# Batch 0 of an attention and mixer kernel: first loads split by token range and head, scores of four heads at a time

## The chip, the cores and the metric

The kernel runs on one core of a Trainium2 chip. The metric is the device time of one execution in microseconds. Engines are named as in the profile: PE does matmuls (PEld is its weight load), DVE works on vectors, ACT on activations, POOL and SP here issue DMAs.

## What is computed

```python
# q, k, v: (8 batches, 8 heads, 576 tokens, 64), f32
scores = scale * np.matmul(q, k.transpose(0, 1, 3, 2))
mask = block_i >= block_j                 # blocks of 64 tokens
attn = softmax(np.where(mask, scores, -1e9))
x = np.matmul(attn, v)                    # then (batch, token, 512)
h = np.maximum(x.T @ w_tok1, 0) @ w_tok2  # mixes tokens, 256 wide
u = x + h.T
out = u + np.maximum(u @ w_ch1, 0) @ w_ch2  # mixes channels, 1536 wide
```

## The kernel before

Every step is an operation of a planner (class `Plan`). `add` records the engines an operation may use, an estimated cost, what it depends on, a priority, an urgency and the PSUM banks that it takes and gives back. `run` then plays a list schedule: at each time the most urgent ready operation of each engine is taken, and none is begun that would run far into a more urgent one that is about to be ready. `search` repeats this 1000 times with randomly moved priorities and keeps the order whose estimated end is earliest. That order becomes the program: each engine executes its instructions strictly in it. The constants in `run` (`soft`, the time from which POOL's loads are taken to move; 0.05 us between dependent operations of one engine) enter this estimate and nothing else.

PSUM has eight banks: four single ones (`mm`, the pool `BANK`) and two pairs (`sc`, the pool `SC`).

Batch 0 starts the kernel, with nothing to overlap. Heads go in two groups of four (hg 0 and 1). For group 0, `load_qk` fetches k and q in f32 by DMAs issued from SP and ACT; the other groups and v come by POOL. Each tensor is fetched as two halves of 288 KB (line 427), each half over all 128 partitions: partition 32h + p holds 18 consecutive tokens of head h, and a half is 9 of them. Each half is cast to bf16 (line 400, on ACT or DVE) and transposed on DVE in 32 x 32 blocks (line 440). Scores of a group need all four transposes, since a half holds every second run of 9 tokens.

`first_attention` goes over four steps: heads 0 and 1, heads 2 and 3 of group 0, then the same of group 1. Each step has three sets of score columns (`SETS`) of 512 columns a head. `score_set` emits the matmuls (line 555), with 32 rows of the array for each head; `exp` turns the two banks of a pair into bf16 weights on ACT (line 574), 1024 elements a partition; `mask` zeroes the blocks that the mask excludes (line 580, DVE). The first of all sets is emitted for four heads, with two of them in single banks, whose exponentials are at line 700. `first_tail` handles the last 64 queries and keys for each step apart (lines 652 and 669). `head_out` multiplies the weights with v (line 602), takes the reciprocal of the sums (624) and normalizes (630).

After that come, for batch 0: `token_up` (788, relu at 774), `first_uT` (817 and 832, copy at 847), `channel_up` (999) and `channel_down` (1311 and 1319). `channel_up` needs all four copies of line 847.

`raise_clock` fills PE before there is work: `WARM` matmuls of 512 columns (line 372), then small ones (line 379) wherever the plan has PE idle before 20 us. `warm_up` runs one exponential on a single column on ACT (line 391), which brings the table load with it.

Of the kernel before, what the change touches and what calls it, by code (L numbers as in the profile page):

```python
# [31 lines left out]
class Plan:  # L32
# [66 lines left out]
    def run(self):  # L99
# [12 lines left out]
        heapq.heapify(queued)  # L112

        avail = {e: [] for e in self.LAG}
        t, hard, soft, gives, order, mode = 0.0, 0.0, 6.2, [], [], 0
        left = len(self.ops)
        landed = [0.0] * 8

# [2 lines left out]
        while left:  # L121
# [13 lines left out]
            for e in ("PE", "ACT", "DVE", "POOL", "SP"):  # L135
# [45 lines left out]
                    heapq.heappush(gives, (o.end + lag * (not o.quick), note["pool"], note["slot"]))  # L181
                for u in o.users:
                    same = u.engines == (e,) and o.xfer is None
                    u.ready = max(u.ready, o.end + (0.05 if same else lag))
                    u.waiting -= 1
                    if not u.waiting:
                        heapq.heappush(queued, (u.ready, u.n))
# [8 lines left out]
def kernel(  # L196
# [11 lines left out]
    nc = tc.nc  # L208
# [75 lines left out]
    P.pool("mm", mm)  # L284
    P.pool("late", [])
    BANK = ("mm", "late")
    WARM, KEEP = 16, 110
    FAST_UP = 4

    def g_of(b):  # L290
# [39 lines left out]
    def act_cost(n):  # L330
        return 0.08 + n * 0.000833
# [57 lines left out]
    def warm_up():  # L389
        def emit(o):  # L390
            nc.scalar.activation(warm, nc.const_aps.tensor(0.0, (128, 1), FP32), EXP)

        P.add("ACT", 1.5, emit, (), -9e3)


    EVAC = ("DVE", "ACT")
# [7 lines left out]
    def load_qk(b, hg, after=[]):  # L404
        i = (2 * b + hg) % 3
        first = b == 0 and hg == 0
        prio = 10 * b + 4 * hg - (100 if b == 0 else 0)
        parts = ((0, NB // 2), (NB // 2, NB))
        done = []
        for n, (src, raw, dst) in enumerate(((k, kraw[i], kT[i]), (q, qraw[i], qT[i]))):  # L410
            hbm = src[b, 4 * hg : 4 * hg + 4].rearrange("h (p k) d -> (h p) (k d)", p=32)
            raw2 = raw.rearrange("p k d -> p (k d)")

            st = stage[0][:, 1152 * n : 1152 * (n + 1)]
            raw_war = reuse(("raw", n, i))
            T_war = reuse(("T", n, i))
            loads = []
            if not first:
                def emit_load(o, hbm=hbm, raw2=raw2):
                    nc.gpsimd.dma_start(out=raw2, in_=hbm)  # L420

                loads = [P.add("POOL", 0.55, emit_load, raw_war, prio + n, xfer=8 * 0.184)]
            for f, (k0, k1) in enumerate(parts):
                if first:
                    def emit_load(o, k0=k0, k1=k1, hbm=hbm, st=st):
                        queue = nc.sync if o.engine == "SP" else nc.scalar
                        queue.dma_start(out=st[:, D * k0 : D * k1], in_=hbm[:, D * k0 : D * k1])

                    ld = P.add(("SP", "ACT")[f % 2], 0.45, emit_load, (), -1e4 + n, xfer=(k1 - k0) * 0.1)

                    def emit_cast(o, k0=k0, k1=k1, raw2=raw2, st=st):
                        cast(o, raw2[:, D * k0 : D * k1], st[:, D * k0 : D * k1])

                    w = D * (k1 - k0)
                    ld = P.add(EVAC, {"ACT": act_cost(w), "DVE": dve_cost(w)}, emit_cast, [ld], -1e4 + 2 + n)
                    reads(("g", 0), ld)
                    loads = [ld]

                def emit(o, raw2=raw2, dst=dst, k0=k0, k1=k1):
                    nc.vector.transpose(  # L440
                        dst[:, 0:S, :]
                        .rearrange("p s e -> p (s e)")
                        .bitcast(I32)
                        .rearrange("p (a k) -> p k a", k=NB)[:, k0:k1],
                        raw2.bitcast(I32).rearrange("p (k a) -> p k a", k=NB)[:, k0:k1],
                    )

                op = P.add("DVE", 0.02 + 32 * (k1 - k0) * 0.00185, emit, loads + T_war + after, prio + 0.1 * n, urgent=(2, 0)[b] if b < 2 else -1)
                reads(("raw", n, i), op)
                done.append(op)  # L450
        return done
# [120 lines left out]
    def exp(dst, n, op, note, prio, urgent=0, give=None):  # L572
        def emit(o):
            nc.scalar.activation(dst, sc[SC.index(note["pool"])][:, :, 0:n], EXP, scale=scale)  # L574

        return P.add("ACT", act_cost(2 * n), emit, [op], prio, give=give or [note], urgent=urgent)

    def mask(e, c, hs, deps, prio, urgent=0):
        def emit(o):
            nc.vector.memset(e[64:128, hs, c : c + 64], 0.0)  # L580

        return P.add("DVE", 0.17, emit, deps, prio, urgent=urgent)

    def head_out(b, head, deps, prio, tail, urgent=0):
        hg, h = divmod(head, 4)

        ei = hg if b == 0 else b % 2
        vt, xt, et, e = v1[b % 2], x_sb[b % 3], et_sb[ei], e_sb[hg]
        shift = 0 if b % 2 == 0 else -64
        bank = {}  # L590

        def emit(o, chunks):
            u = bank_of(bank)[:, 0:330].rearrange("p (i c) -> p i c", c=66)
            for I in chunks:
                for J in range(I + 1):
                    if J < 4:
                        c = ECOL[J] + 128 * (I - J) + (shift if I == 4 else 0)
                        w = e[:, h, c : c + 128]
                    else:
                        c = 64 + 128 * h + (64 * hg if b else 0) + shift  # L600
                        w = et[:, c : c + 128]
                    nc.tensor.matmul(  # L602
                        out=u[:, I, 0:65],
# [36 lines left out]

    TAIL = (512, 512, 64)
    MASKS = ((0,), (576,), (1024, 1344))

    def first_tail(hg, heads, deps, prio):

        notes = [{} for _ in heads]

        def emit(o):
            for par in range(2):
                for h, note in zip(heads, notes):  # L650
                    r = slice(32 * h, 32 * h + 32)
                    nc.tensor.matmul(
                        out=bank_of(note)[:, 0:64],
                        lhsT=kT[hg][r, 512:640, par],
                        rhs=qT[hg][r, 512:576, par],
                        start=(par == 0),
                        stop=(par == 1),
                    )

        op = P.add(  # L660
            "PE", 0.1, emit, deps + pads["kT", hg] + pads["et", hg], prio,
            take=[(BANK, note) for note in notes], mode=1, urgent=2,
        )
        for n in range(2):
            reads(("T", n, hg), op)
        done = {}
        for h, note in zip(heads, notes):
            def emit(o, h=h, note=note):
                nc.scalar.activation(et_sb[hg][:, 64 + 128 * h : 128 + 128 * h], bank_of(note)[:, 0:64], EXP, scale=scale)

            done[h] = P.add("ACT", act_cost(64), emit, [op], -3001, give=[note], urgent=2)
        return done

    def first_attention(ready, v_ready):

        pad = pads["v", 0]
        done = []
        for j in range(4):
            hg, f = divmod(j, 2)
            heads = (2 * f, 2 * f + 1)  # L680
            hs = slice(2 * f, 2 * f + 2)
            e = e_sb[hg]
            prio = -3000 + j
            exps = []
            for n, s in enumerate((2, 1, 0)):
                width = sum(w for _, _, _, w in SETS[s])
                parts = tuple((hg,) + r for r in SETS[s])
                dst = e[:, hs, 512 * s : 512 * s + width]
                if j == 0 and n == 0:

                    note = {}
                    early = [{}, {}]
                    op = score_set(
                        0, parts, range(4), ready[hg], prio - 0.05, [(SC, note)] + [(BANK, x) for x in early]
                    )
                if j == 1 and n == 0:
                    these = []
                    for h, x in zip(heads, early):
                        def emit(o, h=h, x=x, e=e):
                            nc.scalar.activation(e[:, h, 1024:1536], bank_of(x), EXP, scale=scale)  # L700

                        these.append(P.add("ACT", act_cost(512), emit, [op0], prio, give=[x], urgent=2))
                else:
                    if j or n:
                        note = {}
                        op = score_set(0, parts, heads, ready[hg], prio + 0.1 * n, [(SC, note)])
                    else:
                        op0 = op
                    these = [exp(dst, width, op, note, prio + 0.1 * n, urgent=2)]
                if n == (1 if j else 2):  # L710
                    tails = first_tail(hg, heads, [op] + ready[hg], prio + 0.1 * n + 0.05)
                exps += these
                for c in MASKS[s]:
                    exps.append(mask(e, c, hs, these, prio, urgent=1))
            for h in heads:
                deps = exps + v_ready[hg] + pad + pads["e", hg]
                done.append(head_out(0, 4 * hg + h, deps, -2900 + j, tails[h], urgent=1))
        return done

    def attention(b, ready, v_ready):  # L720
# [747 lines left out]
```

## Time and profile before

| what | value |
|---|---|
| median of 3 runs | 294.25 us (293.98 to 295.07) |
| the profiled execution, its time | 294.21 us |
| the profiled execution, its span | 292.4 us |
| PE busy | 286.7 us (98%) |
| DVE busy | 235.7 us (81%) |
| ACT busy | 166.8 us (57%) |
| POOL busy | 62.0 us (21%) |

The span is what the profile sees from the first to the last instruction; the time has 1.8 us around it. Busy PE includes the dummy matmuls and overlapping ends of matmuls, so 98% isn't PE at its peak. In timeline rows the columns are the start in us, the time that the merged instructions cover, the engine, the line, the operation, output and input with their shapes, the count, and in brackets idle time ahead of it with what ended it.

### The profile page before, as it was taken

To read this page: it belongs to the slowest core of one execution; us is meant where nothing else is said; L and a number is where in the kernel's file an instruction comes from. 1 tells how busy PE (TensorE), PEld (TensorE's weight loads), DVE (VectorE), ACT (ScalarE), POOL (GpSimd) and SP (SyncE) were. 2 spreads that over 40 slices of the span, in tenths; PEclk is the share of its full clock that TensorE was granted. 3 is DMA by queue.
4 is the path that set the end of the run, shared out by engine and by line. 5 is a ranking of instruction groups with operands and counts; after the bars stand their busy time and mean duration, and the time that the engine had idled before them with its cause. 6 is when DMAs were issued, how large, how long until landed. Compare 5 with 4: busy or idle time off the path is not lost.

```text
span 292.4 us, 7674 instructions
## 1 busy us (share of the span) xinstructions
PE 286.7 (98%) x3252; PEld 180.4 (62%) x3252; DVE 235.7 (81%) x512; ACT 166.8 (57%) x236; POOL 62.0 (21%) x96
## 2 busy tenths in 40 slices
PE   8999999999999999999999999999999999999994
PEld 3666445554558765555774657775446885566883
DVE  5566668988959979959997979668998968969993
ACT  5797874576777563786656796433477004867000
POOL 8765454710430170170031000000000000000000
PEclk9999999999999999999999999999999999999999
DMA  8999999994794299995329012041000911130054
GB/s 213 186 172 211 210 181 185 231 190 112 115 128 75 43 164 198 166 131 62 73 16 211 5 34 40 2 151 49 3 0 11 152 72 74 36 143 4 0 183 145
DMA packets 64403, 31.99 MB, mean 109 GB/s; under 512 B 53104, under 2 KB 55024, under 8 KB 64368
## 3 DMA queue, kind: packets, MB, share of 16 engines
q0 software_dynamic: 44320, 17.34, 50.6%
q1 hardware_dynamic: 19760, 13.57, 17.4%
q10 hardware_dynamic: 288, 0.59, 0.6%
q8 instruction: 25, 0.41, 0.6%
q14 instruction: 10, 0.08, 0.1%
HBM read 35.85 MB, written 9.44 MB: 155 GB/s over the span
## 4 chain that ended last, share of the span: by engine, by line
PE 93%; ACT 4%; DVE 1%; issue 0%
PE mm L1228 18%; PE mm L999 15%; PE sc L555 9%; PE mm L602 9%; PE mm L1319 7%; PE mm L1104 6%; PE late L1104 6%; PE mm L788 6%; PE late L1228 4%; PE mm L881 4%; ACT e_sb L574 4%; PE mm L1026 3%; PE mm L372 2%; DVE turned L440 1%; PE mm L912 1%; PE mm L379 0%
## 5 line engine op out<-in xcount | busy, mean ns | idle before, releaser
L574 ACT ACTIVATE e_sb<-sc 128x1024 bf16<-128x1024 f32 x95 | 92.6, 1031 | 33.0 <-PE sc L555 29.8
L999 PE MATMUL mm<-uT,wc_sb 128*128 128x512 bf16 x192 | 46.1, 382 | 0.0
L440 DVE STREAM_TRANSPOSE turned<-raws 128x288 int32<-128x288 int32 x64 | 40.2, 705 | 3.4 <-ACT raws L400 1.5
L469 POOL DMA_DIRECT2D vals<-in_v_dram x45 | 36.9, 837 | 26.8 <-PE mm L602 22.4
L555 PE MATMUL sc<-turned 32*128 32x64 bf16 (+4 forms) x744 | 35.4, 281 | 0.6 <-ACT e_sb L574 0.4
L602 PEld LDWEIGHTS <-e_sb 128*128 128x128 bf16 x896 | 31.3, 97 | 6.7 <-issue 3.2
L999 PEld LDWEIGHTS <-wc_sb 128*128 128x128 bf16 x192 | 20.0, 115 | 20.8 <-issue 5.5
L602 PE MATMUL mm<-vals,e_sb 128*128 128x65 bf16 x868 | 32.5, 193 | 0.0
L630 DVE TENSOR_TENSOR x_sb<-mm,rinv 128x320 bf16<-128x320 f32 x62 | 29.1, 485 | 1.3
L1228 PEld LDWEIGHTS <-sums 128*128 128x128 bf16 x252 | 24.1, 98 | 4.4 <-issue 1.2
L776 DVE TENSOR_SCALAR gT<-mm 128x512 bf16<-128x512 f32 x27 | 18.5, 687 | 10.1 <-PE mm L999 10.0
L1228 PEld LDWEIGHTS <-gT 128*128 128x128 bf16 x240 | 22.9, 98 | 4.5 <-issue 1.3
L555 PEld LDWEIGHTS <-turned 32*128 32x128 bf16 x752 | 12.6, 93 | 18.9 <-issue 16.3
L400 ACT COPY e_sb<-mm 128x512 f32<-128x512 f32 x14 | 8.2, 593 | 26.6 <-PE mm L1104 25.0
L774 ACT ACTIVATE gT<-mm 128x512 bf16<-128x512 f32 x24 | 14.4, 598 | 10.9 <-PE mm L999 10.8
L580 DVE MEMSET e_sb<- 64x128 uint32 (+1 forms) x72 | 10.6, 153 | 9.3 <-ACT e_sb L574 5.2
L788 PE MATMUL mm<-x_sb,w_sb 128*128 128x512 bf16 (+1 forms) x102 | 17.9, 316 | 0.0
L420 POOL DMA_DIRECT2D raws<-in_k_dram x15 | 8.2, 549 | 40.3 <-DVE turned L440 30.6
L896 DVE TENSOR_TENSOR u_sb<-mm,x_sb 128x512 bf16<-128x512 f32 x24 | 15.4, 682 | 1.4 <-PE mm L881 1.3
L1251 DVE TENSOR_TENSOR o_sb<-mm,u_sb 128x512 f32<-128x512 f32 x20 | 13.7, 686 | 3.4 <-PE mm L1228 2.6
L1228 PE MATMUL mm<-wd_sb,sums 128*128 128x256 bf16 x132 | 15.7, 273 | 0.0
L1251 DVE TENSOR_TENSOR o_sb<-mm,o_sb 128x512 f32<-128x512 f32 (+1 forms) x19 | 12.0, 631 | 4.4 <-PE mm L1228 4.2
(146 smaller groups left out, 458.7 us busy)
## 6 DMA issues: line engine op xcount, KB each, us to landing
out_dram<-o_sb SPq DMA_DIRECT2D x14, 512.0 KB, 3.1
raws<-in_k_dram POOLq DMA_DIRECT2D x15, 288.0 KB, 6.9
raws<-in_q_dram POOLq DMA_DIRECT2D x15, 288.0 KB, 7.5
vals<-in_v_dram POOLq DMA_DIRECT2D x28, 128.0 KB, 6.8
wc_sb<-in_moe_w_ch_dram POOLq DMA_DIRECT2D x8, 192.0 KB, 6.6
wc_sb<-in_moe_w_ch_dram POOLq DMA_DIRECT2D x3, 512.0 KB, 10.9
out_dram<-o_sb SPq DMA_DIRECT2D x10, 128.0 KB, 2.3
vals<-in_v_dram POOLq DMA_DIRECT2D x15, 64.0 KB, 5.8
```

The costliest lines, as they stand in the source:

```text
L440: nc.vector.transpose(dst[:, 0:S, :] .rearrange("p s e -> p (s e)") .bitcast(I32) .rearrange("p (a k) -> p k a", k=NB)[:, k0:k1], raw2.bit ...
L469: nc.gpsimd.dma_start(out=dst, in_=src)
L555: nc.tensor.matmul(out=home(n)[:, c0 : c0 + w], lhsT=kT[i][r, j0 : j0 + 128, par], rhs=qT[i][r, i0 : i0 + w, par], start=(par == 0), stop= ...
L574: nc.scalar.activation(dst, sc[SC.index(note["pool"])][:, :, 0:n], EXP, scale=scale)
L602: nc.tensor.matmul(out=u[:, I, 0:65], lhsT=w, rhs=vt[:, J, head, 0:65], start=(J == 0), stop=(J == I),)
L630: nc.vector.tensor_tensor(out=xt[:, :, 64 * head : 64 * head + 64], in0=u[:, :, 0:64], in1=ri.to_broadcast([128, 5, 64]), op=MULT,)
L788: nc.tensor.matmul(out=bank_of(bank)[:, w * n : w * n + w], lhsT=wt[:, tt : tt + 255 : 2], rhs=xt[:, c, cols], start=(c == 0), stop=(c == 4),)
L999: nc.tensor.matmul(out=bank_of(bank), lhsT=wc1_sb[:, m, channels(cc)], rhs=uT[b % 2][:, :, m, :], start=(m == 0), stop=(m == NDM - 1),)
L1104: nc.tensor.matmul(out=bank_of(bank), lhsT=x(m), rhs=y[:, :, m, :], start=first and m == 0, stop=m == 1, skip_group_check=not first,)
L1228: nc.tensor.matmul(out=bank_of(bank)[:, 256 * i : 256 * i + 256], lhsT=x[:, kk, 128 * i : 128 * i + 128], rhs=y[:, kk], start=first and i ...
L1251: nc.vector.tensor_tensor(out=dst, in0=src, in1=other, op=ADD)
L1319: nc.tensor.matmul(out=ps, lhsT=gt[:, cc, c0 : c0 + 128], rhs=wc2_sb[:, cc, cols], start=(cc == 0 and not turned), stop=(cc == NDC - 1),)
```

## The change

Loads of batch 0's first group: k goes by SP, q by ACT. The token range is cut at 256 (8 x 32) instead of by alternating runs of 9. Each part is fetched head by head: 4 pieces of 64 KB for tokens 0 to 255, then 4 pieces of 80 KB for tokens 256 to 575, so 16 DMAs for 4. The casts have urgency 3 and wait for four pieces. The transposes of the first part write tokens 0 to 255 only, so scores of the first 256 tokens can be computed before the rest is there.

Scores: nine sets, nearly all for four heads at once, with the results in pairs (`SC`), in single banks (`BANK`, whose exponentials are done head by head by `single`) or both. The tails of both groups are one set. Group 1 has another order of columns (`ECOL_LAST`), so that its last two sets (heads 0 and 1, then 2 and 3) hold columns that need no mask. The exponentials of the tails go to one buffer, `et_sb[0]`, as in the other batches.

Besides, `WARM` is 12 instead of 16, the warm-up exponential may start at 0.75 at the earliest, and a few constants of the planner's estimate are changed.

```diff
-        t, hard, soft, gives, order, mode = 0.0, 0.0, 6.2, [], [], 0
+        t, hard, soft, gives, order, mode = 0.0, 0.0, 5.0, [], [], 0
-                    u.ready = max(u.ready, o.end + (0.05 if same else lag))
+                    u.ready = max(u.ready, o.end + ((e != "PE") * 0.05 if same else lag))
-    WARM, KEEP = 16, 110
+    WARM, KEEP = 12, 110
-        P.add("ACT", 1.5, emit, (), -9e3)
+        P.add("ACT", 1.5, emit, (), -9e3, at=0.75)
-        parts = ((0, NB // 2), (NB // 2, NB))
+        parts = ((0, 8), (8, NB)) if first else ((0, NB // 2), (NB // 2, NB))
...
-                        queue.dma_start(out=st[:, D * k0 : D * k1], in_=hbm[:, D * k0 : D * k1])
-
-                    ld = P.add(("SP", "ACT")[f % 2], 0.45, emit_load, (), -1e4 + n, xfer=(k1 - k0) * 0.1)
+                    pieces = []
+                    for h in range(4):
+                        def emit_load(o, h=h, k0=k0, k1=k1, heads=heads, st=st):
+                            queue = nc.sync if o.engine == "SP" else nc.scalar
+                            piece = heads[h, 32 * k0 : 32 * k1, :].rearrange("(p k) d -> p (k d)", p=32)
+                            queue.dma_start(out=st[32 * h : 32 * h + 32, D * k0 : D * k1], in_=piece)
+
+                        pieces.append(P.add(("SP", "ACT")[n], 0.42, emit_load, (), -1e4 + f, xfer=0.02, at=0.7))
...
-                    ld = P.add(EVAC, {"ACT": act_cost(w), "DVE": dve_cost(w)}, emit_cast, [ld], -1e4 + 2 + n)
+                    ld = P.add(EVAC, {"ACT": act_cost(w), "DVE": dve_cost(w)}, emit_cast, pieces, -1e4 + 2 + f, urgent=3)
...
-        return P.add("ACT", act_cost(2 * n), emit, [op], prio, give=give or [note], urgent=urgent)
+        return P.add("ACT", act_cost(2 * n) - 0.02, emit, [op], prio, give=give or [note], urgent=urgent)
...
-        return P.add("DVE", 0.17, emit, deps, prio, urgent=urgent)
+        return P.add("DVE", 0.12 if urgent else 0.17, emit, deps, prio, urgent=urgent)
...
+    ECOL_LAST = (448, 0, 1024, 1344)
+
+    def first_attention(ready, v_ready):
...
+        def four(parts, n, dst, deps, prio, masks=(), homes=(SC, SC)):
+            notes = [[{}] if f is not BANK else [{}, {}] for f in homes]
+            pools = [(pool, x) for pool, xs in zip(homes, notes) for x in xs]
+            op = score_set(0, parts, range(4), deps + seen, prio, pools)
+            seen[:] = [op]
...
+        e0, e1 = e_sb
+        four(((0, 0, 0, 0, 256),), 256, e0[:, :, 0:256], [k0, q0], -3000.0, (0,))
+        four(((0, 0, 0, 256, 256),), 256, e0[:, :, 256:512], [k0, q0, q1], -2999.9, (), (BANK, BANK))
+        four(((0,) + SETS[1][0], (0,) + SETS[1][1]), 512, e0[:, :, 512:1024], ready[0], -2999.8, MASKS[1])
+        four(((0,) + SETS[2][0], (0,) + SETS[2][1]), 512, e0[:, :, 1024:1536], ready[0], -2999.7, MASKS[2], (SC, BANK))
+        four(
+            ((0, 0) + TAIL, (1, 64) + TAIL), 128, et[:, 64:576].rearrange("p (h c) -> p h c", h=4), every, -2999.6,
+            (), (SC, BANK),
+        )
+        four(
+            ((1,) + SETS[2][0], (1,) + SETS[2][1]), 512, e1[:, :, 1024:1536], later, -2998.9, MASKS[2],
+            (SC, BANK),
+        )
+        four(
+            ((1, 0, 128, 128, 448), (1, 448, 0, 0, 64)), 512, e1[:, :, 0:512], later, -2998.8, (0, 448),
+            (SC, BANK),
+        )
+        note = {}
+        op = score_set(0, ((1, 0, 0, 64, 512),), (0, 1), later + seen, -2998.7, [(SC, note)])
+        exps[1][0].append(exp(e1[:, 0:2, 512:1024], 512, op, note, -2998.7, urgent=2))
+        ends = [{}, {}]
+        op = score_set(0, ((1, 0, 0, 64, 512),), (2, 3), later + [op], -2998.6, [(BANK, x) for x in ends])
+        last = [single(e1[:, 2 + i, 512:1024], 512, op, x, -2998.6 + 0.01 * i) for i, x in enumerate(ends)]
```

## The prediction, made before the result was known

> **What bounds the kernel now.** I read the page first: PE is busy 98% of the 292.4 us span, so after a start-up the kernel is a matmul stream. The granted clock is full throughout. The change rewrites batch 0 alone, so I then asked for the chain of waits in the first 30 us.
>
> ```profile
> 1.19 5.83 PE mm L372 x16
> 7.02 1.42 PE mm L379 x13
> ...
> 9.04 1.90 ACT e_sb L574 x2
> ...
> 11.34 1.05 ACT e_sb L574
> ...
> 14.26 2.75 ACT e_sb L574 x3
> 17.01 0.23 ACT vals L669 x2
> 17.24 1.84 ACT e_sb L574 x2
> ...
> 27.27 2.71 PE mm L999 x12
> ```
>
> Columns: start, length, what. Lines 372 and 379 are dummy matmuls, so the first 8.4 us hold no useful PE work. From 9.04 the exponentials on ACT end last. From about 20 us it is PE again, and L999 (channel-up of batch 0) opens the stretch where PE never stops. So a microsecond off the first L999 is about a microsecond off the end, as long as the loads keep up. The timeline gives the steps:
>
> ```profile
> 4.86 2.57 ACT L400 CAST raws<-gT 128x576 bf16<-128x576 f32 x4 [1.71 <-DMA gT<-in_k_dram]
> ...
> 5.56 2.62 DVE L440 STREAM_TRANSPOSE turned<-raws 128x288 int32<-128x288 int32 x4 [1.49 <-ACT raws L400]
> ...
> 8.37 0.23 PE L555 MATMUL sc<-turned 32*128 32x64 bf16 x4
> ...
> 20.01 1.14 ACT L574 ACTIVATE e_sb<-sc 128x1024 bf16<-128x1024 f32 x1
> ...
> 23.84 0.49 DVE L630 TENSOR_TENSOR x_sb<-mm,rinv 128x320 bf16<-128x320 f32 x1
> ...
> 25.91 1.24 ACT L847 CAST uT<-mm 128x512 bf16<-128x512 f32 x2
> ```
>
> Three stretches follow. Before: loads land, four casts, four transposes, first scores at 8.37, first exponential at 9.04. Middle: ACT runs without a hole worth naming until the last exponential ends at 21.15. After: last head's product, its normalization (ends 24.33), the token mix, the last uT copy (ends 27.15), L999 at 27.20. The last stretch is 27.20 - 21.15 = 6.05 us.
>
> **What the Trainium skill says.** TensorEngine Tiling (Array Packing), section Key Properties: tiles of the array work independently. The trace agrees: a pass of two heads over 512 columns takes as long as one of four.
>
> ```profile
> 12.46 0.62 PE L555 MATMUL sc<-turned 32*128 32x512 bf16 x4
> ...
> 29.91 0.63 PE L555 MATMUL sc<-turned 32*128 32x512 bf16 x8
> ```
>
> ScalarE: Activation LUTs, section What ACT_TABLE_LOAD costs: 1283 ns for the load, which is this trace's duration too, and back-to-back ACTIVATEs overlap. The chain agrees on the second: three 1024-element exponentials in 2.75 us are 0.917 each, though the mean of one is 1031 ns. DMA: Bandwidth & Descriptors, section Anatomy of one DMA: a fixed part of about 2 us. The trace agrees roughly: 128 KB stores land in 2.3 us.
>
> **The change, part by part.**
>
> *Loads.* Before, SP and ACT issue two transfers of 288 KB each; they land 4.1 to 5.2 us after issue, all by 1.20 + 5.2 = 6.4. After, each issues eight pieces, four of 64 KB (tokens 0 to 255), then four of 80 KB. The pitch of an issue is 0.43 us (0.74, 1.17). The fourth issue starts at 0.74 + 3 x 0.43 = 2.03, the eighth at 3.75, and it ends at 4.2. Pieces land about 2.3 us after issue (the nearest size, 128 KB): first part 4.4, second 6.1. A hidden limit may bind:
>
> ```profile
> 9.09 0.54 POOL L488 DMA_DIRECT2D w_sb<-in_moe_w_tok_dram  x1 [0.74 <-DMA raws<-in_k_dram]
> ```
>
> This is POOL's eleventh DMA, and it waited for the third: at most eight are outstanding. No row shows whether SP and ACT together have such a limit. If they have, the ninth issue waits for the first to land (about 3.0), the sixteenth for the eighth (4.4): second part at 6.7, and ACT is held until 4.8. Bounds: 0 to 0.6 us; I take 0.6, since POOL's queue shows it.
>
> *Table load.* It sat at 1.65, in the shadow of the loads. Now eight issues precede it on ACT until 4.2, and the planner's rule (nothing that runs into a more urgent operation) puts the warm-up behind the first cast. Table and warm-up are 1.28 + 0.20 = 1.48 us; what queues behind them is the second-part cast and the exponentials. If the load comes before the cast instead, it delays that by up to 1.28. I take it after the cast.
>
> *Casts and transposes.* One first-part cast goes to each of ACT (about 0.5 by the pitch 2.57/4 less 10%) and DVE (no SBUF cast on DVE in the trace; bounded by 0.2 and 0.68, the PSUM copy of 512 elements; I take 0.6). ACT: 4.8 to 5.35. DVE: cast 4.5 to 5.1, then two transposes of 256 elements, 0.56 each (0.63 pitch x 256/288), so 6.35 with the gap to the cast. Scores of set 1 need one more pass of 256 columns: done at 6.75. ACT: warm-up 5.35 to 6.85, a 640-element cast to 7.45. First exponential about 7.5 instead of 9.04: 1.5 earlier. DVE then casts the second part's q (from 6.7) and transposes q to about 8.2 and k to 8.9, so sets 2 and 3 follow with some 0.3 us of holes.
>
> *Warm-up matmuls 16 to 12.* Until 5.43 weights come every 0.427 us, then twice as fast. Ten cold and two fast ones end near 5.9, so set 1 isn't blocked at 6.4; sixteen ended at 7.02 and would block it.
>
> *Exponentials.* From the chain, 1024 elements cost 0.917, 512 cost 0.49, and 64 cost 0.115: 0.063 + 0.000833 per element. Before: 11 of 1024, 2 of 512, 8 of 64, that is 21 x 0.063 + 12,800 x 0.000833 = 11.99. After: the same 12,800 elements in 23 instructions, 12.11. So ACT gains nothing here; last exponential at 7.5 + 12.1 + 0.3 = 19.9 instead of 21.15. The 16 mask memsets stay 16; all but the last sets' stay beside ACT.
>
> *Scores.* Before, ten two-head sets of 0.57, a four-head one and four tails of 0.27: 7.35 us of PE. After: six of 0.57 and three of 0.3, 4.3. The 3 us saved lie beside ACT, and only help where PE is behind.
>
> *The end of batch 0.* All of group 0 finishes about 6.4 us after the first exponential (6,656 elements in 14 instructions), near 14.0. The remaining PE work is fixed: eight heads at 0.45, token-up 4 x 0.56, identity passes 4 x 0.22, mixing 4 x 0.43 = 8.46 us. Four-head sets take two of the four single banks each, so I let the first head start at 15.3 when set 6 frees its banks, and one or two score passes still lie between: about 9.3, so 24.6, plus the last copy: 25.2. From the other side: set 8 frees heads 4 and 5 two singles (0.98) before the end, set 9 then heads 6 and 7. DVE takes 0.70 per head (0.20 + 0.49); four heads in a row end at 19.9 + 2.5 = 22.4, and from last multiply to L999 was 27.20 - 24.33 = 2.87: 25.3. The two agree at 25.2, so L999 comes 2.0 us earlier. The unmasked last set saves the wait from 21.15 to 21.55 that the last memset made.
>
> *What is late next.* At 26.63 PE had done one score pass of batch 1 (0.57) before L999; its k released a waiting POOL load when it landed, at 23.05, and its transposes can't be much earlier, so it moves behind L999. Gain 1.4 to 2.0; I take 1.8. Weights: the last channel-up load is issued at 20.21 and takes 6.6, so 26.8; its first user is the fifth group, 3.6 us after L999, 28.8. The first channel-down load (23.05 + 10.9 = 34.0) has its user at 37.82 - 2 = 35.8. Both hide.
>
> *Planner constants* (exponential and mask costs, PE latency, start of soft loads) change the order of everything after, through a random search. No row prices that; from a PE that is never idle between 27 and 287 I bound it at 0.8 us either way and take 0.
>
> **Sum.** The profiled execution was 294.21 with a span of 292.4, next to a median of 294.25. 294.21 - 1.8 = 292.4.
>
> **Rivals.** *The front is gated* (0.22): the limit of eight, and the table load in front of the cast, put the first exponential at 8.3. Then 8.3 + 12.1 + 0.5 = 20.9, plus 5.3 is 26.2, less the moved pass: gain 0.4, 293.8. For it: 16 issues instead of 4, and ACT waits for every one. Against: the first part is small and both queues send it first.
>
> *More than forecast* (0.14): pieces land faster, first exponential at 6.9, no holes, and PE, freed of 3 us of scores, has no backlog: 19.0 + 4.9 = 23.9, gain 3.3: 290.9. Against: ACT's queue, table included, leaves little room below 7.
>
> *Slower* (0.15): the four-head sets starve the heads of banks. Each of sets 4 to 7 and 9 takes two of four single banks at higher urgency than any head's product. If the first product slips, 8.46 + 0.57 (a score pass) + 0.65 (the last copy) = 9.7 us lies behind it. The point from which it loses is 27.2 - 9.7 = 17.5; at 19.1 L999 is at 28.8, which is 1.6 later: 295.8. For it: the first head needs all of group 0, 13.09 before. Against: banks free at every single, 0.49 apart.
>
> **How the numbers follow.** Forecast 0.49, own range 291.0 to 293.4; rivals 0.22, 0.14, 0.15. A measurement of this kernel can tell about 0.5%, or 1.47 us, from no change. Faster than 292.8: 0.41 of the forecast, 0.14, and 0.03 of the gated case, 0.58. Slower than 295.7: 0.14. The rest, 0.28. The range 290.3 to 295.2 takes in the 0.8 of the reordering and leaves out the far ends of the large gain and of the slower case.
>
> **What would show it.** Right: first exponential of scores at 7.2 to 7.9, ACT without holes to about 20, first L999 near 25.2, and the end moved by as much. Wrong: a first cast after 5.5 or a table load ahead of it (gated), first L602 after 17 with ACT done (starved), or an early L999 followed by waits on weight loads.

## The result, and the profile after

| kernel | median | lowest to highest | runs |
|---|---|---|---|
| before | 294.57 us | 293.98 to 295.07 | 6 |
| after | 301.70 us | 301.59 to 301.99 | 6 |

The ratio is 1.0245 with a 95% interval of 1.023 to 1.0259: slower by 7.1 us, where 1.8 us less (292.4) was forecast. The profiled execution of after took 301.59 us, with a span of 299.8.

The chain of waits of after, at the places that answer to those shown of before (start, length, what):

```profile
2.14 5.62 DMA gT<-in_q_dram
...
7.78 5.55 DMA gT<-in_q_dram
...
16.25 2.54 PE mm L379 x13
...
34.70 2.71 PE mm L996 x12
```

L996 is before's L999, the first channel-up. It starts at 34.70 where before had 27.27. From there to the end of the span before needed 265.1 us and after 265.1 as well. So all 7.4 us were lost ahead of it. The chain also says where to look: the last q piece on ACT could not be issued before 7.78, when an earlier piece landed, and both of them needed 5.6 us from issue to landing.

The timeline of ACT in after, where the bracket is the idle time before a row and what ended it, and one row of PE:

```profile
0.74 7.35 ACTq L431 DMA_DIRECT2D gT<-in_q_dram  x8
8.13 1.28 ACT L400 ACT_TABLE_LOAD   x1 [8.13 <-DMA gT<-in_q_dram]
9.42 0.62 ACT L400 CAST raws<-gT 128x512 bf16<-128x512 f32 x1
...
13.26 0.73 ACT L400 CAST raws<-gT 128x640 bf16<-128x640 f32 x1 [3.12 <-DMA gT<-in_k_dram]
13.89 1.08 ACT L581 ACTIVATE e_sb<-sc 128x512 bf16<-128x512 f32 x2
...
27.02 1.16 ACT L683 ACTIVATE e_sb<-mm 128x512 bf16<-128x512 f32 x2
```

```profile
10.76 0.41 PE L562 MATMUL sc<-turned 32*128 32x256 bf16 x8 [4.02 <-DVE turned L446]
```

ACT is held by its eight issues until 8.1. The table load comes only then, ahead of the first cast. The second casts wait for data until 13.26, and the first exponential starts at 13.89 instead of 9.04. The last one ends at 28.18 instead of 21.15. The loss is there before the exponentials (4.85 us), grows by 2.2 us in their phase, and by 0.4 us behind it.

The PE row is the first score set, which needs the first 256 tokens alone. It was done at 11.17, and ACT was free from 10.15. But in ACT's fixed order the cast of the second part stands ahead of the first exponential, so that exponential waited for the second part all the same. The two exponentials of this set take 1.08 us; by this estimate no more than about 1 us could have been drawn forward by another order. No run tries one.

The DMA view of after's first 20 us (KB of one transfer, then median us from issue to landing; q10 is one of the two queues of SP and ACT: packets, MB, share of the 16 DMA engines) gives the landing of both parts, and the same view of before the landing of two of its four transfers:

```profile
q10 hardware_dynamic: 384, 0.59, 10.1%
...
gT<-in_k_dram SPq DMA_DIRECT2D x4, 80.0 KB, 5.7
gT<-in_q_dram ACTq DMA_DIRECT2D x4, 80.0 KB, 5.9
...
gT<-in_k_dram SPq DMA_DIRECT2D x4, 64.0 KB, 2.6
```

```profile
gT<-in_k_dram ACTq DMA_DIRECT2D x1, 288.0 KB, 4.1
...
gT<-in_q_dram SPq DMA_DIRECT2D x1, 288.0 KB, 5.2
```

Before, transfers of 288 KB landed 4.1 to 5.2 us after issue; these of 80 KB take longer than the large ones did. The median of the 64 KB pieces hides a spread. Asked one by one, the first pieces, issued at 0.74, landed after 2.0 and 2.3 us, ahead of POOL's first load (issued at 1.44). The fourth, issued at 2.11 and 2.14, took 5.4 and 5.6.

### The profile page after: what moved, and what is told of

Same layout as the page of the kernel before. It is cut to its first block, busy times and chain, and to the rows that moved or that the text cites. A ratio compares the mean times of both kernels' runs of the same rounds, so it can differ in the third digit from the quotient of the medians.

```text
span 299.8 us, 7777 instructions
## 1 busy us (share of the span) xinstructions
PE 287.3 (96%) x3276; PEld 181.9 (61%) x3276; DVE 232.2 (77%) x507; ACT 168.8 (56%) x243; POOL 62.4 (21%) x96
## 4 chain that ended last, share of the span: by engine, by line
PE 91%; DMA 4%; DVE 3%; ACT 1%; issue 0%; ACTq 0%; DVEq 0%
PE mm L1225 18%; PE mm L996 15%; PE sc L562 9%; PE mm L610 9%; PE mm L1316 7%; PE late L1101 6%; PE mm L1101 6%; PE mm L785 5%; DMA gT<-in_q_dram 4%; PE late L1225 4%; PE mm L1023 3%; PE mm L878 3%; PE mm L379 2%; DVE u_sb L893 1%; PE late L878 1%; PE mm L909 1%
## 5 line engine op out<-in xcount | busy, mean ns | idle before, releaser
L581 ACT ACTIVATE e_sb<-sc 128x1024 bf16<-128x1024 f32 (+1 forms) x92 | 88.8, 1015 | 31.5 <-PE sc L562 30.8
L996 PE MATMUL mm<-uT,wc_sb 128*128 128x512 bf16 x192 | 45.8, 382 | 0.0
L446 DVE STREAM_TRANSPOSE turned<-raws 128x288 int32<-128x288 int32 (+2 forms) x64 | 40.2, 704 | 2.8 <-ACT raws L400 1.4
L562 PE MATMUL sc<-turned 32*128 32x64 bf16 (+5 forms) x732 | 32.8, 281 | 4.3 <-DVE turned L446 4.0
L996 PEld LDWEIGHTS <-wc_sb 128*128 128x128 bf16 x192 | 20.1, 115 | 20.1 <-issue 4.9
L771 ACT ACTIVATE gT<-mm 128x512 bf16<-128x512 f32 x36 | 21.6, 601 | 8.4 <-PE mm L996 5.9
L400 ACT COPY e_sb<-mm 128x512 f32<-128x512 f32 x12 | 7.1, 588 | 29.1 <-PE mm L1101 29.1
L773 DVE TENSOR_SCALAR gT<-mm 128x512 bf16<-128x512 f32 x16 | 11.0, 689 | 15.5 <-PE mm L996 12.4
L1248 DVE TENSOR_TENSOR o_sb<-mm,u_sb 128x512 f32<-128x512 f32 x22 | 15.1, 687 | 2.4 <-PE mm L1225 2.2
L785 PE MATMUL mm<-x_sb,w_sb 128*128 128x512 bf16 (+1 forms) x98 | 16.6, 314 | 0.0
L1248 DVE TENSOR_TENSOR o_sb<-mm,o_sb 128x512 f32<-128x512 f32 (+1 forms) x19 | 12.3, 648 | 4.8 <-PE mm L1225 4.4
L1101 PEld LDWEIGHTS <-raws 128*128 128x128 bf16 x96 | 9.3, 98 | 10.2
L632 DVE RECIPROCAL rinv<-mm 128x5 f32<-128x5 f32 x63 | 11.4, 187 | 5.1 <-PE mm L610 3.9
```

Of the source, the lines that this page charges most:

```text
L446: nc.vector.transpose(dst[:, t0:t1, :] .rearrange("p s e -> p (s e)") .bitcast(I32) .rearrange("p (a k) -> p k a", k=nk)[:, ks], raw2.bitc ...
L562: nc.tensor.matmul(out=home(n)[:, c0 : c0 + w], lhsT=kT[i][r, j0 : j0 + 128, par], rhs=qT[i][r, i0 : i0 + w, par], start=(par == 0), stop= ...
L771: nc.scalar.activation(dst, src, RELU)
L785: nc.tensor.matmul(out=bank_of(bank)[:, w * n : w * n + w], lhsT=wt[:, tt : tt + 255 : 2], rhs=xt[:, c, cols], start=(c == 0), stop=(c == 4),)
L996: nc.tensor.matmul(out=bank_of(bank), lhsT=wc1_sb[:, m, channels(cc)], rhs=uT[b % 2][:, :, m, :], start=(m == 0), stop=(m == NDM - 1),)
L1101: nc.tensor.matmul(out=bank_of(bank), lhsT=x(m), rhs=y[:, :, m, :], start=first and m == 0, stop=m == 1, skip_group_check=not first,)
```

## The experiments

Every kernel here computes the whole of the reference. The kernel before was run beside each; its median there is given in brackets.

After the result the theory was: the loads make the whole loss. Sixteen small transfers land late beside POOL's loads, and each queue's fifth to eighth (the ninth to sixteenth of all) wait for its first to fourth to land. The rivals were: the table load ahead of the casts; the four-head sets and the new order; and the clock of PE, which the windows view shows below full speed.

**e1_old_loads.** After, with before's four transfers; all sets then wait for all transposes of group 0.

```diff
-        parts = ((0, 8), (8, NB)) if first else ((0, NB // 2), (NB // 2, NB))
+        parts = ((0, NB // 2), (NB // 2, NB))
...
-                    for h in range(4):
...
+                    def emit_load(o, k0=k0, k1=k1, hbm=hbm, st=st):
+                        queue = nc.sync if o.engine == "SP" else nc.scalar
+                        queue.dma_start(out=st[:, D * k0 : D * k1], in_=hbm[:, D * k0 : D * k1])
...
-        four(((0, 0, 0, 0, 256),), 256, e0[:, :, 0:256], [k0, q0], -3000.0, (0,))
-        four(((0, 0, 0, 256, 256),), 256, e0[:, :, 256:512], [k0, q0, q1], -2999.9, (), (BANK, BANK))
+        four(((0, 0, 0, 0, 256),), 256, e0[:, :, 0:256], ready[0], -3000.0, (0,))
+        four(((0, 0, 0, 256, 256),), 256, e0[:, :, 256:512], ready[0], -2999.9, (), (BANK, BANK))
```

> The changed kernel with the loads of before: four transfers of 288 KB, alternating runs of 9 tokens, all four transposes ahead of the first scores. Theory (the sixteen small transfers make the loss, the rest of the change gains): 291 to 294.5 us, first L996 at 25 to 27. Rival (the four-head score sets and their use of banks cost time themselves): 297 or more, first L996 after 29.

Measured: 293.72 us over 12 runs [294.26], ratio 0.999 (0.9973 to 1.0006). The loads make the whole loss, and the rest of the change, alone, is not to be told from nothing. Two timelines of this kernel say why it isn't a gain, ACT's and PE's:

```profile
21.67 1.09 ACT L676 ACTIVATE e_sb<-mm 128x512 bf16<-128x512 f32 x2 [0.30 <-PE mm L555]
```

```profile
21.01 0.62 PE L555 MATMUL mm<-turned 32*128 32x512 bf16 x4
...
27.39 2.78 PE L989 MATMUL mm<-uT,wc_sb 128*128 128x512 bf16 x12
```

The last exponential ends at 22.76, so the stretch from there to the first channel-up (L989 here) is 4.63 us, against 6.05 before. But it ends 1.6 us later than before's: its matmuls come at 21.01 only, and ACT waited for PE three times on the way (0.21 to 0.30 us each). What the tail gave back was lost among the exponentials.

**e2_new_loads_alone.** Before, with after's `load_qk`: the loads, casts and transposes of the change without the rest of it.

```diff
-                        queue.dma_start(out=st[:, D * k0 : D * k1], in_=hbm[:, D * k0 : D * k1])
...
+                            piece = heads[h, 32 * k0 : 32 * k1, :].rearrange("(p k) d -> p (k d)", p=32)
+                            queue.dma_start(out=st[32 * h : 32 * h + 32, D * k0 : D * k1], in_=piece)
```

> The kernel before with the sixteen pieces and nothing else of the change in its attention. Theory: 299 to 303 us, second parts landing near 13 again. Rival (score sets cost): 294 to 297.

Measured: 302.59 us [294.26], ratio 1.0279 (1.0249 to 1.0309). The loss comes with the loads alone. ACT's timeline:

```profile
0.74 1.28 ACT L391 ACT_TABLE_LOAD   x1 [0.74 <-PEq L1459]
...
13.36 0.72 ACT L400 CAST raws<-gT 128x640 bf16<-128x640 f32 x1 [0.82 <-DMA gT<-in_q_dram]
```

Here the table load comes first, and the last cast is as late as in after. So the place of the table load is not the cause.

**e3_whole_parts.** After, with each token part of a tensor in one transfer: four transfers, the same token cut.

```diff
-                    for h in range(4):
...
-                            piece = heads[h, 32 * k0 : 32 * k1, :].rearrange("(p k) d -> p (k d)", p=32)
-                            queue.dma_start(out=st[32 * h : 32 * h + 32, D * k0 : D * k1], in_=piece)
+                        piece = heads[:, 32 * k0 : 32 * k1, :].rearrange("h (p k) d -> h p (k d)", p=32)
+                        queue.dma_start(out=st[:, D * k0 : D * k1], in_=piece)
```

> The changed kernel with each part in one transfer over 128 partitions (256 and 320 KB, four in all), so the cut by token ranges stays. Theory: the first part lands by 5.2 and the second by 6.6, first exponential of scores at 7.2 to 7.8, 290.5 to 293.5 us. Rival (reading by token ranges is slow in itself, since a head's part isn't next to another head's): the first part lands after 7, 297 or more.

**e4_eight_pieces.** The same with two heads in a transfer: eight transfers.

```diff
-                    for h in range(4):
+                    for h in (0, 2):
...
-                            piece = heads[h, 32 * k0 : 32 * k1, :].rearrange("(p k) d -> p (k d)", p=32)
-                            queue.dma_start(out=st[32 * h : 32 * h + 32, D * k0 : D * k1], in_=piece)
+                            piece = heads[h : h + 2, 32 * k0 : 32 * k1, :].rearrange("h (p k) d -> h p (k d)", p=32)
+                            queue.dma_start(out=st[32 * h : 32 * h + 64, D * k0 : D * k1], in_=piece)
```

> The changed kernel with pieces of two heads: eight transfers of 128 and 160 KB, so that none is a ninth. If the wait of the ninth for the first makes most of the loss: second part lands by 7.5, 291 to 294.5 us. If each small transfer is slowed by the loads beside it: the first part lands after 7, the second after 9, 296 to 299.

Measured: 305.66 us [294.26], ratio 1.0386 (1.0354 to 1.0418), and 320.95 us, ratio 1.0906 (1.0869 to 1.0942). Both are slower than after. For e3 the rival named 297 or more; for e4 neither case had foreseen it. The transfer that landed last in each, from the two chains, e3 first:

```profile
1.55 17.15 DMA gT<-in_k_dram
```

```profile
2.77 28.37 DMA gT<-in_k_dram
```

The queue's packets say what happened. First e3 in its first 30 us, then before in its first 20:

```profile
q10 hardware_dynamic: 264, 0.59, 6.0%
```

```profile
q10 hardware_dynamic: 288, 0.59, 8.9%
```

All move the same bytes: two transfers of 128 rows are 256 packets. Before has 32 more, 16 for each of its two transfers on that queue; e3 has 8 more, 4 for each; e4 has 264 as well, over four transfers, 2 for each; after has 384, 16 for each of eight. The Trainium skill, DMA: Bandwidth & Descriptors, section Why a DMA increments its semaphore by 16 and not by 1, says that each engine taking part reports once, and that the slowest dimension of the access pattern sets how many take part (the largest number up to 16 that divides it on both sides). The counts agree: an outer dimension of four heads gives 4 engines, two heads give 2, rows of 32 or 128 partitions give 16. So these two runs don't test how many transfers are best. They test a narrow transfer, at 17 and 28 us. They can't be held for or against either theory, e3's rival (reading by token ranges is slow in itself) included.

**e5_pool_held.** After, with all of POOL's loads behind two copies that read the first casts. That takes POOL's traffic away from the first pieces and leaves their number and their wait as they are.

```diff
+                    if f == 0:
+                        def emit_gate(o, raw2=raw2, n=n):
+                            nc.gpsimd.tensor_copy(gate[:, n : n + 1], raw2[:, 0:1])
+
+                        held_loads.append(P.add("POOL", 0.1, emit_gate, [ld], -9e5))
...
-                op = P.add("POOL", 0.66 + 0.02 * nh, emit, sw, prio, xfer=p * nh / 16 * (0.0175 if staged else 0.013))
+                op = P.add("POOL", 0.66 + 0.02 * nh, emit, sw + held_loads, prio, xfer=p * nh / 16 * (0.0175 if staged else 0.013))
```

> The changed kernel, sixteen pieces and all, with two copies of one column put ahead of POOL's loads; they read the casts of the first part, so no POOL load moves beside the first pieces. If the pieces are slow because POOL's loads move beside them: each lands 2.0 to 2.5 us after its issue, first part by 4.7, eighth issue before 5, first exponential of scores at 7 to 8.5, and 292 to 297 us (POOL's loads start some 4 us late). If small pieces are slow by themselves: first part after 7 again, above 301.

Measured: 300.73 us [294.64], ratio 1.0226 (1.0186 to 1.0265). The total hardly moves and misses the 292 to 297 of the first case, but the front does what that case says. (The profiled execution was the slowest of the four, 303.01 us, with PE at half clock from 20 to 25 us; the rows of the front are ahead of that.) SP's last issue in the timeline, and the landing of such pieces in the DMA view of 4.6 to 5.2 us:

```profile
4.96 0.31 SPq L433 DMA_DIRECT2D gT<-in_k_dram  x1
```

```profile
gT<-in_k_dram SPq DMA_DIRECT2D x2, 80.0 KB, 2.9
```

Its ACT timeline:

```profile
7.95 0.73 ACT L402 CAST raws<-gT 128x640 bf16<-128x640 f32 x1 [0.36 <-DMA gT<-in_k_dram]
8.65 1.08 ACT L588 ACTIVATE e_sb<-sc 128x512 bf16<-128x512 f32 x2
...
21.05 0.28 ACT L690 ACTIVATE vals<-mm 128x128 bf16<-128x128 f32 x1 [6.03 <-PE mm L569]
```

Without POOL's loads beside them all sixteen pieces land in 2.3 to 3.0 us, where in after those that end the two parts took 5.4 to 5.6, and the first exponential comes 5.2 us earlier than in after, earlier than in before. So the number of pieces alone doesn't make them slow; POOL's traffic beside them does. The wait of the ninth is still there, and SP's last issue stands at 4.96 (ACT's at 5.23) where an issue behind the other would have been at 3.75: 1.2 us, or 1.5. The first exponential, at 8.65, is about as much behind the 7.5 forecast. But POOL's first load is at 7.79 instead of 1.44, group 1 arrives late, and ACT then stands idle for 6.03 us before the joint tails, which need both groups. The first channel-up is at 35.53 in this execution. Holding all of POOL's loads this long gives back what the front gains; a shorter hold was not tried.

**e6_whole_heads.** After, without the token cut: one transfer of 144 KB for each head of k and of q, eight in all, so that there is no ninth, and 32 rows in each, so that each runs on 16 engines (192 packets on a queue: 128 rows, and 16 for each of four).

```diff
+            for h in range(4) if first else ():
+                def emit_load(o, h=h, heads=heads, st=st):
+                    queue = nc.sync if o.engine == "SP" else nc.scalar
+                    piece = heads[h].rearrange("(p k) d -> p (k d)", p=32)
+                    queue.dma_start(out=st[32 * h : 32 * h + 32], in_=piece)
```

> The changed kernel with a whole head (32 partitions, 144 KB) in each transfer: eight transfers that the hardware spreads as it does the small ones, none a ninth, no cut by token ranges, casts and transposes as before. If the ninth's wait for the first is most of the loss: all land by 7.5, 293 to 296.5 us. If being small beside POOL's loads is most of it: the last lands after 9, 297 to 301.

Measured: 298.16 us [294.64], ratio 1.0122 (1.009 to 1.0155). The DMA view of its first 12 us:

```profile
gT<-in_q_dram SPq DMA_DIRECT2D x2, 144.0 KB, 6.0
gT<-in_q_dram ACTq DMA_DIRECT2D x2, 144.0 KB, 6.2
```

Nothing is held: all are issued by 2.6. Still q lands after 6.0 to 6.2 us, later than q's 288 KB before (5.0 and 5.2), and k after 3.6 to 3.9. By the ratios, eight transfers of 144 KB cost 3.9 us more than four of 288 KB (1.0122 against 0.999, of 294.4), with no ninth and no token cut in it. The order was searched anew, and the four executions lie between 297.24 and 299.37, so the 3.9 is rough.

**e7_warm34.** After, with 34 warming matmuls instead of 12, to keep PE's clock up until the first scores.

```diff
-    WARM, KEEP = 12, 110
+    WARM, KEEP = 34, 110
```

> The changed kernel with 34 warm-up matmuls instead of 12, which end near 10.5, so that PE does not idle between 6.7 and 10.8. If the halved clock from 10 to 18 us makes a part of the loss: clock full there, first L996 at 32.5 to 34 instead of 34.7, 299.5 to 301 us. If it makes none: 301.2 to 302.2.

Measured: 299.13 us [294.64], ratio 1.0155 (1.0134 to 1.0177). The last exponential ends at 28.26, as in after (28.18), but the first channel-up starts at 32.92 instead of 34.64. `WARM` is also an input of the search, and this order has token-up earlier (24.75 instead of 29.12). The granted clock fell all the same (0.67 from 15 to 20 us), after PE had been idle for 3.78 us before 14.52. So the run doesn't answer for the clock. It shows instead that with the last exponential at the same place another order moves the first channel-up by 1.7 us.

**e8_sixteen_same_plan.** e1, with each of its four load operations sending four transfers of one head. The plan, and so every engine's order, is e1's.

```diff
-                        queue.dma_start(out=st[:, D * k0 : D * k1], in_=hbm[:, D * k0 : D * k1])
+                        for h in range(4):
+                            r = slice(32 * h, 32 * h + 32)
+                            queue.dma_start(out=st[r, D * k0 : D * k1], in_=hbm[r, D * k0 : D * k1])
```

> The kernel of e1 with each of its four loads written as four transfers of one head's 32 partitions, where it stood; every engine's other instructions keep the order of e1, so nothing but the sixteen transfers differs. If being small beside POOL's loads and the wait of each ninth transfer for the first add up: k lands near 7.5, q near 13, 300 to 304 us. If the wait adds nothing to being small: all land by 9.5 as in e6, 297 to 299.

Measured: 303.34 us [294.6], ratio 1.0304 (1.029 to 1.0318). Its ACT timeline:

```profile
3.43 4.45 ACTq L429 DMA_DIRECT2D gT<-in_q_dram  x4
...
13.71 1.25 ACT L400 CAST raws<-gT 128x576 bf16<-128x576 f32 x2 [3.18 <-DMA gT<-in_q_dram]
16.41 1.09 ACT L576 ACTIVATE e_sb<-sc 128x512 bf16<-128x512 f32 x2 [1.45 <-PE sc L557]
```

One row of its PE timeline, and one of its windows view (columns as under e9; the number after the busy times is the granted clock):

```profile
36.66 2.78 PE L991 MATMUL mm<-uT,wc_sb 128*128 128x512 bf16 x12
```

```profile
15.00:20.00 5.00, 3.73 (x40) 2.02 (x40) 3.38 (x9) 3.57 (x8) 4.47 (x9) 0.50 1.55 191
```

The same bytes, the same order (POOL's loads too, with the same starts up to 5.7), the same rows in SBUF, before's runs of tokens, only in sixteen transfers: 9.2 us more than e1 by the ratios, and the first channel-up at 36.66 instead of 27.39. This is the cleanest of the runs, and it shows that the cut by token ranges isn't needed for the loss. The four issues of q span 4.45 us, since each waits for a landing, and the last casts come at 13.71. The first exponential is 7.1 us later than in e1 (16.41 against 9.33). The other 2.2 us come among the exponentials, where PE, idle for 7.51 us before its first scores, runs at half clock. As in e9 the clock is the likely reason; no run of e8 holds it.

**e9_same_plan_warm.** After, with 28 more warming matmuls sent by the same operation; the plan doesn't know of them, so every order stays as it is.

```diff
-            for _ in range(WARM):
+            for _ in range(WARM + 28):
```

> The changed kernel with 28 more warm-up matmuls put behind the 12, and the order of every engine otherwise as it was; PE is busy to about 12.9. If the halved clock costs time: clock full until 15 at least, the thirteen dummies from 16.2 take 1.5 us instead of 2.5, first L996 0.8 to 2 us earlier, 299.7 to 301. If the chain was set by ACT and the loads alone: within 0.4 of 301.7.

Measured: 300.49 us [294.6], ratio 1.0205 (1.019 to 1.022). The windows view (stretch, length, busy time and count of PE, PEld, DVE, ACT, POOL, then the granted clock, the DMA share and GB/s), after and then e9:

```profile
10.00:15.00 5.00, 2.34 (x25) 1.42 (x27) 2.15 (x4) 1.85 (x5) 3.89 (x6) 0.65 1.25 214
15.00:20.00 5.00, 5.00 (x60) 3.08 (x53) 3.06 (x9) 3.68 (x8) 3.59 (x7) 0.67 1.65 181
```

```profile
10.00:15.00 5.00, 4.65 (x47) 2.91 (x48) 1.86 (x4) 1.71 (x3) 3.82 (x6) 1.00 1.21 218
15.00:20.00 5.00, 4.98 (x87) 3.51 (x76) 3.21 (x11) 4.81 (x10) 3.85 (x7) 1.00 1.70 185
```

And e9's PE timeline:

```profile
15.63 1.64 PE L379 MATMUL mm<-wd_sb 128*128 128x256 bf16 x13
```

In after, PE was idle from 6.73 to 10.76 for want of data, and the clock of the two stretches was 0.65 and 0.67. These are averages: asked for stretches of 1 us, the same view of after has 0.50 in each from 12 to 18, and 1.00 again from 19. The Trainium skill, TensorE: Matmul & The Clock Gate, section What's actually happening, has it that an idle window of about 3.4 us sends PE to half clock. The trace agrees, with 4.02 us of idling and then 0.50. With the clock held, the thirteen dummies in the middle take 1.64 us instead of 2.61, the first exponential stays where it was (13.85), the last ends at 26.65 instead of 28.18, and the time is 1.2 us less. So about 1.2 of the 7.1 us are the halved clock: a consequence of the late loads.

**e10_last_pair.** e1, with the last score set in one pair of banks and one exponential, instead of two single banks and two.

```diff
-        ends = [{}, {}]
-        op = score_set(0, ((1, 0, 0, 64, 512),), (2, 3), later + [op], -2998.6, [(BANK, x) for x in ends])
-        last = [single(e1[:, 2 + i, 512:1024], 512, op, x, -2998.6 + 0.01 * i) for i, x in enumerate(ends)]
+        note = {}
+        op = score_set(0, ((1, 0, 0, 64, 512),), (2, 3), later + [op], -2998.6, [(SC, note)])
+        last = [exp(e1[:, 2:4, 512:1024], 512, op, note, -2998.6, urgent=2)] * 2
```

> The kernel of e1 with the last score set (heads 2 and 3 of group 1) in a pair of banks instead of two single ones, with one exponential of 1024. If the last set was late in e1 (matmuls at 21.01, 0.3 us of idle ACT before its exponentials) because products and token-up held the single banks: last exponential ends at 21.5 to 22.2 instead of 22.76, first channel-up 0.4 to 1.2 us earlier than 27.39, 292.5 to 293.4 us. If it was late because of PE's order alone: within 0.3 of 293.7.

Measured: 293.27 us over 5 runs [294.6], ratio 0.9963 (0.9949 to 0.9977), the fastest of all kernels here. Its ACT and PE timelines:

```profile
20.17 1.08 ACT L574 ACTIVATE e_sb<-sc 128x1024 bf16<-128x1024 f32 x1
```

```profile
26.77 2.78 PE L989 MATMUL mm<-uT,wc_sb 128*128 128x512 bf16 x12
```

The last exponential follows the one before it without a hole and ends at 21.25, 1.5 us earlier than in e1 (0.4 of it is there at the first exponential, 8.93 against 9.33); the first channel-up is 0.6 us earlier. The gain on before is 1.1 us by the ratio: small, though its interval leaves out 1. The interval of e1 overlaps it. Its order was searched anew too, so the bank is the likely reason and not a proven one.

## Why the prediction was wrong, step by step

**The step that failed** is the sentence "Pieces land about 2.3 us after issue (the nearest size, 128 KB): first part 4.4, second 6.1". The row was of stores in the middle of the kernel. In e5, without POOL's loads beside them, the pieces do land in 2.3 to 3.0 us. In after, beside POOL's loads, which start at 1.44, the fourth piece of each queue takes 5.4 to 5.6 and the eighth 5.6: first part 7.5 and 7.8, second 13.1 and 13.3. A duration was taken by size; it should have been taken by company. The better row stands in the prediction itself: 288 KB in 4.1 to 5.2 us, in the same place and also beside POOL's loads. By it the fourth piece, issued at 2.03, would land at 6.1 to 7.2, when the large transfers are there too (by 6.4), so an estimate from this row leaves nothing to gain. What in POOL's traffic slows a small transfer so was not taken apart and stays open.

**The limit of eight** was put at 0 to 0.6 us. A limit exists: each queue's fifth to eighth issue falls on the landing of its first to fourth. Both queues issue in step here, so a limit of four each would look like one of eight together; no run tells them apart. Its price is not a constant. With quick landings it is 1.2 to 1.5 us (e5). With slow ones the wait and the landing follow one another, 5.6 + 5.6 us in the chain, and the last issue goes from 3.75 to 7.78. The sixteen transfers cost 9.2 us (e8 against e1); eight without a ninth cost 3.9 (e6 against e1), so the other 5.3 come with the ninth to sixteenth, their waits and their number together, and with the halved clock, which e8 has and e6 has not (1.00 from 5 to 20 us): its part is put at no more than the 2.2 us lost among e8's exponentials. e6's order was searched anew, which by e7 can be worth over a microsecond, so this split is rough.

**The table load** was taken behind the first cast; it came ahead of it, at 8.13, and the trace puts it at the cast's own line (L400). By itself that cost nothing here, because the chain runs through the last pieces and DVE's cast at 13.45.

**Casts.** DVE's cast of 512 elements took 0.43 us (0.6 taken), ACT's 0.62 (0.5 taken, though 2.57/4 less 10% is 0.58). No part of the error.

**Warm-up matmuls.** Twelve end in time, as said. That PE would then be idle long enough to lose half its clock wasn't thought of: 1.2 us.

**Exponentials and scores.** ACT's 12.11 us and "holes 0.3" gave 12.4; e10 takes 21.25 - 8.93 = 12.3. After needs 14.3, with waits for PE of 0.47, 0.88 and 0.36 us, behind matmuls that ran at half clock until 18; with the clock held (e9) it is 12.8. A four-head pass costs what a two-head pass does, as predicted (in e1 a set of four heads and 512 columns runs from 15.55 to 16.18, and one of two heads takes 0.62).

**The tail** from the last exponential to the first channel-up was put at 5.3; e10 has 5.5, e1 4.63, after 6.5. (The fixed PE work in it adds up to 8.44 us and not 8.46, which changes nothing.) The mechanism was right, and in e10 it shows; but the same trace has the first exponential at 8.93, not at 7.5, since the old loads land as before.

**From the first channel-up to the end** one for one: +7.4 there, +7.1 in the time. In e1 and e10 the first channel-up stands at +0.2 and -0.4, and their spans (291.7 and 291.4) at -0.7 and -1.0, so there the rule holds to within 0.9 us. It fails in e2: +12.1 at the first channel-up (39.26), +8.9 in the span. Later loads hid, as said.

**The search** was bounded at 0.8 us for "everything after", and taken at 0. From the first channel-up to the end before needed 265.2 us, after 265.2, and e1 and e5 to e10 264.3 to 266.2, so the bound was nearly right there; in e2 (262.0) it was too small. The order inside batch 0 had no term: e7 has 1.7 us at the first channel-up from another order.

**The rivals.** "The front is gated" had the right place and both signs that it named (first cast after 5.5, table load ahead of it). Its 8.3 for the first exponential against 13.89 measured shows that it used the same 2.3 us a piece. "Slower: banks" had the right sign and the wrong cause. In e1 there is a mild form of it (the last set late at 21.01), which e10 removes. Without the new loads it never made the kernel slower than before. "More than forecast" asked for pieces that land faster still, and they landed later.

## What to carry to other kernels

Price a transfer from a row with the same neighbours on the DMA engines, not from one of the same size: beside the same POOL loads four transfers of 288 KB gave their data by 6.4 us (e1), and the same bytes in sixteen pieces by 13.7 (e8). Cutting a first load to start earlier did not pay in any run here. Pieces beyond the number that may be outstanding waited one landing more (after, e8), pieces on 4 or 2 engines took 17 and 28 us (e3, e4), and even eight pieces free of both cost time (e6). Look at the fixed order too: what is to start early must not stand behind what comes late. And when a front gets later, look for what goes cold behind it: PE, idle for 4 us, ran at half its clock from 12 to 18 us.

## What was not expected of the hardware

- A transfer with an outer dimension of four or two heads ran, by its packets, on 4 or 2 DMA engines (264 packets instead of 288 or 384) and took up to 17 us for 320 KB and 28 us for 160 KB.
- Beside POOL's loads the transfers that ended a part took 5.4 to 6.7 us (64 to 144 KB; after and e6); with POOL held, those of 64 and 80 KB took 2.3 to 3.0. The Trainium skill, DMA: Bandwidth & Descriptors, section Rules for kernel authors, says not to split a transfer over halves of the partitions but to use one over all 128. The runs agree: 293.7, 298.2 and 303.3 us for 4, 8 and 16 transfers of the same bytes (e1, e6, e8; e6 with another order).
- In after, PE was granted half its clock in each us from 12 to 18, after 4.02 us without work.
- The fifth to eighth issue of SP's and of ACT's queue each waited for the landing of that queue's first to fourth (after, e5, e8).
